# Two linear-attention and two gated layers on one core: adjacent token rows per partition, a new start, and an instruction order given by a table

## The chip, the cores and the metric

The kernel runs on one core of a Trainium2 chip. The metric is the time of one execution on the device in microseconds (us). A core has five engines, each with its own queue that is worked in order: TensorE (PE; its weight loads are PEld), VectorE (DVE), ScalarE (ACT), GpSimd (POOL) and SyncE (SP), which here issues most DMAs.

## The reference

```python
x = A_x                                              # 1 x 2048 x 512, bf16
x = x + _A_ref(_layernorm(x), wqkv, w_phi, wo)       # linear attention, 32 heads of 16
x = x + _B_ref(_layernorm(x), W_gate, W_up, W_down)  # gated layer, 1376 hidden columns
x = x + _A_ref(...)                                  # the same weights once more
x = x + _B_ref(...)

# _A_ref
pq, pk = q @ w_phi, k @ w_phi                        # per head
phi_q = concat([softmax(pq), softmax(-pq)])          # phi_k in the same way, of pk
kv, z = phi_k^T v, sum over tokens of phi_k
o = (phi_q kv) / (phi_q z + 1e-6);  return o @ wo
# _B_ref
gate = gate * (gate > 0);  return (gate * up) @ W_down
```

Nothing in it depends on the order of the tokens: the layer norm, the projections and the gated layer work row by row, and the attention sums over all rows.

## The kernel before, in words

The 2048 tokens are 16 tiles of 128 rows; x stays in SBUF in `x_sb` from the load to the store. `build_kernel` doesn't emit instructions in program order. It records each step as an operation (`Program.op`, L59) with its engine, the data it reads and writes, and two assumed durations, and then calls `schedule` (L299). That function gives each operation a priority (`tails`, L120: the longest chain behind it), plays all five queues forward (`forward`, L129: among the operations that could start within 60 ns, the one of the highest priority goes first), derives new priorities by a backward pass, does so 8 times and keeps the order with the smallest assumed length. DMAs have assumed costs as well (L52, L53). `prepare` (L314) turns the order into semaphore waits, and `emit` writes each engine's queue. So a change to an assumed cost can move instructions everywhere. At run time each queue is worked in the order thus fixed.

The start: DVE builds an identity matrix (L444 to L459). Partition p of `x_sb` holds rows p, 128 + p, and so on (`xv`, in the view `b (t p) d`). The key weights are loaded in four blocks (L494), transposed on TensorE (L527), copied out of PSUM (L532, L534), multiplied by a block-diagonal form BD of w_phi (L518, L542) and copied to `Wkp` (L546, L548), so that one projection gives pk. The same is done for the queries (`Wqp`), whose transposed weights come by four DMA transposes (L485) on SP. Five matmuls on a zeroed tile (L514) stand at the head of TensorE's queue.

The layer norm `ln` takes statistics on DVE (L559, L560), the reciprocal root as ln and exp on ACT (L562, L564), and y = normalised x on DVE (L579) or, for tiles 4 to 15 of the first layer (`POOL_Y`), on POOL (L574, L576). y is transposed either on TensorE with a copy by ACT (L588, L591; the tiles in `PE_Y`) or by a DMA transpose on SP (L594). `kv_tile` makes K (L612), two exponentials on ACT (L617), their sums z on DVE (L618), their reciprocals (L622, L623 on ACT or L625 on DVE), the product on DVE (L626), and V (L635) with its copy on ACT (L638). `kv_sums` multiplies phi_k and V over all tiles (L671), and DVE takes the wanted blocks (L679, L682). `q_chunk` makes Q (L651) and its exponentials (L655). `attn_tile` makes the attention of a tile: the product with the sums (L704), the denominators over ACT (L718, L727, L728) and POOL (L725, L726, L729), the scaling on DVE (L738, L743, L747), the transpose (L753 or a DMA, L759), the projection (L764) and the addition to x (L767). The gated layer makes gate and up columns (L794), the relu on ACT (L801), the product hT on DVE (L802), a remainder of 96 columns (`rem`, L822 to L831), and the down projection (L846, L848) with the addition to x (L852). Tiles of the last layer are stored by SP (L854). All eight PSUM banks are one pool, handed out by `forward`.

SP's queue at the start holds, in this order: the four key blocks, x tiles 2 and 3, the value weights, x tiles 4 to 7, the four weight transposes, x tiles 8 to 11, x tiles 12 to 15, and then the y transposes. ACT issues x0, w_phi and x1.

Of the kernel before, what the change touches and what calls it, by code (L numbers as in the profile page):

```python
# [10 lines left out]
P = 128  # L11
# [38 lines left out]
class Program:  # L50
    SYNC = 40.0
    DMA_ISSUE, DMA_FIXED, DMA_BW = 520.0, 1500.0, 230.0  # L52
    TR_ISSUE, TR_FIXED, TR_TIME = 1250.0, 1050.0, 250.0  # L53

    def __init__(self, n_dma_sems=64):
        self.ops = []
        self.n_dma_sems = n_dma_sems
# [41 lines left out]


# [12 lines left out]
    def lat(self, o):  # L113
        if o.dma == "tr":
            return self.TR_ISSUE + self.TR_FIXED + self.TR_TIME
        if o.dma:
            return self.DMA_ISSUE + self.DMA_FIXED + o.nbytes / self.DMA_BW
        return o.lat

    def tails(self):  # L120
        tail = [0.0] * len(self.ops)
        for o in reversed(self.ops):
            best = self.lat(o)
            for s, data in o.succ:
                best = max(best, tail[s.i] + (self.lat(o) + self.SYNC if data else self.busy(o)))
            tail[o.i] = best
        return tail

    def forward(self, prio, look=60.0):  # L129
# [4 lines left out]
        for o in ops:  # L134
            o.npend = len(o.deps) + len(o.order)
            o.ready = 0.0
            o.prio = prio[o.i]
            for t in o.tiles:
                tiles[id(t)] = t
# [3 lines left out]
        free = dict.fromkeys(ENGINES, 0.0)  # L143
# [32 lines left out]
        while left:  # L176
# [45 lines left out]
            if o.dma == "tr":  # L222
                free[e] = st + self.TR_ISSUE
                bus = max(bus, free[e]) + self.TR_TIME
                o.end = bus + self.TR_FIXED
            elif o.dma:
                free[e] = st + self.DMA_ISSUE
                bus = max(bus, free[e]) + o.nbytes / self.DMA_BW
                o.end = bus + self.DMA_FIXED
            else:  # L230
                free[e] = st + o.ii
                o.end = st + o.lat
# [66 lines left out]
    def schedule(self, rounds=12):  # L299
        self.links()  # L300
        prio = self.tails()
        best = None
        self.log = []
        for k in range(rounds):
            m = self.forward(prio)
            self.log.append(m)
            if best is None or m < best[0]:
                best = (m, prio)
            prio = self.backward([o.start for o in self.ops])
        self.forward(best[1])  # L310
        return best[0]
# [66 lines left out]
def build_kernel(nc, A_x, A_wqkv, A_w_phi, A_wo, B_x, B_W_gate, B_W_up, B_W_down, out):  # L378
# [8 lines left out]
    def sb(name, shape, dt=BF16):  # L387
        return E(nc.sbuf_tensor(name, [P] + list(shape), dt))
# [13 lines left out]
    rowi, coli, colf = sb("rowi", [32]), sb("coli", [32]), sb("colf", [1], FP32)  # L402
# [41 lines left out]
    op("dve", lambda e: e.memset(wm.ap(), 0.0), writes=[c_warm], ii=150, lat=210, name="warm")  # L444
    op("dve", lambda e: e.memset(ident[:], 0.0), writes=[c_id], ii=60, lat=100, name="id0")
    op("dve", lambda e: e.memset(rowi[:, 0:1], 0.0), writes=[c_row], ii=30, lat=70, name="row0")
    for k in range(5):
        n = 1 << k
        op("dve", lambda e, n=n: e.tensor_scalar(rowi[:, n:2 * n], rowi[:, 0:n], float(n), None, ALU.add), reads=[c_row], writes=[c_row], ii=70, lat=150, name="row")
    op("dve", lambda e: e.transpose(coli[:], rowi[:]), reads=[c_row], writes=[c_col], ii=100, lat=215, name="col")  # L450
    c_colf = res("colf")
    op("dve", lambda e: e.tensor_copy(colf[:], coli[:, 0:1]), reads=[c_col], writes=[c_colf], ii=70, lat=150, name="colf")
    c_idq = [res("identq", q) for q in range(4)]
    for q in range(4):
        sl = slice(32 * q, 32 * q + 32)
        op("dve", lambda e, sl=sl: e.tensor_scalar(ident[sl, sl], rowi[sl, :], colf[sl, :], None, ALU.is_equal), reads=[c_row, c_colf, c_id], writes=[c_idq[q]], ii=75, lat=150, name="identq")
    c_id = c_idq
    op("dve", lambda e: e.tensor_reduce(m8[:], ident[:].rearrange("p (h d) -> p h d", d=16), AX.X, ALU.add), reads=c_id, writes=[c_m8], ii=200, lat=290, name="m8")
    op("dve", lambda e: e.tensor_reduce(mask2[:].rearrange("p (a b) -> p a b", b=2), ident[:].rearrange("p (a f b) -> p a b f", f=16, b=2), AX.X, ALU.add), reads=c_id, writes=[c_m2], ii=200, lat=290, name="mask2")  # L459
    op("dve", lambda e: e.memset(eps[:], 1e-5), writes=[c_eps], ii=35, lat=70, name="eps")  # L460
    va_all = p_va.slots
    for i in range(16):
        op("pool", lambda e, i=i: e.memset(va_all[i][:, :, 128:130], 1.0), writes=[res("va1", i)], ii=60, name="vones")
    for i in range(2):
        op("pool", lambda e, i=i: e.memset(p_hr.slots[i], 0.0), writes=[res("hr0", i)], ii=500, name="hr0")
    op("pool", lambda e: e.tensor_copy(kvs[:, :, 136:144], mask2[:].unsqueeze(1).to_broadcast([P, 8, 8])), reads=[c_m2], writes=[res("kvsm")], ii=200, lat=280, name="kvsm")


    xv = A_x.rearrange("b (t p) d -> p (b t) d", p=P)
    outv = out.rearrange("b (t p) d -> p (b t) d", p=P)  # L470
# [13 lines left out]
    def load_wT(dst, rr, col, ic):  # L484
        o = op("sp", lambda e: e.dma_start_transpose(dst.ap()[:, :, ic * 128:(ic + 1) * 128], A_wqkv[ic * 128:(ic + 1) * 128, col:col + 512]),  # L485
               writes=[rr[ic]], dma="tr", nbytes=131072, name=f"wT{col}.{ic}", after=chain["sp"][-1:])
        chain["sp"].append(o)
# [5 lines left out]
    def load_wk(ic):  # L493
        load("sp", lambda e: e.dma_start(wk_n[ic][0].ap(), A_wqkv[ic * 128:(ic + 1) * 128, 512:1024]), [wk_n[ic][1]], 131072, f"wk{ic}")  # L494
    load_x("act", 0, 1)
    load_wk(0)
    load("act", lambda e: e.dma_start(w128[:], A_w_phi.rearrange("(c h) d f -> (h d) c f", c=4)), [c_w128], 16384, "wphi")
    load_wk(1)
    load_wk(2)
    load_x("act", 1, 2)  # L500
    load_wk(3)
    load_x("sp", 2, 4)
# [5 lines left out]
    load_x("sp", 8, 12)  # L508
    load_x("sp", 12, 16)
# [3 lines left out]
    for k in range(5):  # L513
        op("pe", lambda e: e.matmul(pt_w.ap(), wm.ap()[:, 0:128], wm.ap(), start=True, stop=True), reads=[c_warm], writes=[r_w], ii=430, lat=600, name="warm")  # L514


    for a in range(4):
        op("dve", lambda e, a=a: e.tensor_tensor(BD[:].rearrange("p c (a f b) -> p c a f b", f=16, b=2)[:, :, a], w128[:].unsqueeze(3).to_broadcast([P, 4, 16, 2]),  # L518
                                                 m8[:, 2 * a:2 * a + 2].unsqueeze(1).unsqueeze(1).to_broadcast([P, 4, 16, 2]), ALU.mult),
           reads=[c_w128, c_m8], writes=[c_BD[a]], ii=190, lat=280, name="BD")  # L520

    for ic in range(4):
        pt, pres = tile(p_ps, "WkT", ic)

        def mmt(e, ic=ic, pt=pt):
            for c in range(4):
                i = e.transpose(pt.ap().bitcast(BF16)[:, c * 128:(c + 1) * 128], wk_n[ic][0].ap()[:, c * 128:(c + 1) * 128], ident[:])  # L527
            return i
        op("pe", mmt, reads=[wk_n[ic][1]] + c_id, writes=[pres], ii=240, lat=400, name="WkT mm")
        src = lambda pt: pt.ap().bitcast(BF16)[:, 0:512].rearrange("p (c n) -> p c n", c=4)  # L530
        if ic % 2:
            op("act", lambda e, ic=ic, pt=pt: e.activation(t_wk.ap()[:, :, ic * 128:(ic + 1) * 128], src(pt), ACT.Copy), reads=[pres], writes=[c_wkT[ic]], ii=477, lat=580, name="WkT cp")  # L532
        else:
            op("dve", lambda e, ic=ic, pt=pt: e.tensor_copy(t_wk.ap()[:, :, ic * 128:(ic + 1) * 128], src(pt)), reads=[pres], writes=[c_wkT[ic]], ii=340, lat=420, name="WkT cp")  # L534
# [15 lines left out]
    r_wk = compose(t_wk, c_wkT, Wkp, "Wkp", ["act", "dve", "act", "dve"])  # L550
# [5 lines left out]
    def ln(l, ts):  # L556
# [9 lines left out]
        for t in ts:  # L566
# [6 lines left out]
            if (l, t) in POOL_Y:  # L573
                op("pool", lambda e, t=t: e.tensor_scalar(nmr[:, t, :], mv[:, t, 0:1], rstd[:, t, :], -1.0, ALU.mult, ALU.mult), reads=[res("mv", t), res("rstd", t)], writes=[res("nmr", t)],  # L574
                   ii=100, lat=170, name=f"nmr{l}.{t}")
                op("pool", lambda e, t=t, yt=yt: e.tensor_scalar(yt.ap(), x_sb[:, t, :], rstd[:, t, :], nmr[:, t, :], ALU.mult, ALU.add), reads=[res("x", t), res("nmr", t), res("rstd", t)],  # L576
                   writes=[yr], claims=[dst], ii=1000, lat=1050, name=f"yp{l}.{t}")
# [15 lines left out]
            else:  # L593
                op("sp", lambda e, yt=yt, dst=dst, c=c: e.dma_start_transpose(dst.ap()[:, :, c:c + 128], yt.ap()), reads=[yr], writes=[rr],  # L594
                   dma="tr", nbytes=131072, name=f"yT{l}.{t}")
# [5 lines left out]
    def kv_tile(l, t):  # L601
# [12 lines left out]
        kop[l, t] = op("pe", mmk, reads=[rr] + r_wk, writes=[kr], claims=[ft], ii=864, lat=1030, name=f"K{l}.{t}")  # L614
# [73 lines left out]
    def attn_tile(l, t):  # L688
# [69 lines left out]
        else:  # L758
            op("sp", lambda e: e.dma_start_transpose(oT_.ap(), ot_.ap()), reads=[or_], writes=[oTr], dma="tr", nbytes=131072, name=f"oT{l}.{t}")  # L759
# [46 lines left out]
    def rem(l, s):  # L806
# [7 lines left out]
        for k in range(2):  # L814
# [17 lines left out]
           dma="tr", nbytes=131072, name=f"remT{l}.{s}")  # L832
# [24 lines left out]
    for g in ([0], [1], [2], [3], [4, 5], [6, 7], [8, 9, 10, 11], [12, 13, 14, 15]):  # L857
        ln(0, g)
    for t in range(NT):
        kv_tile(0, t)  # L860
    last_tr = [o for o in pr.ops if o.name.startswith("yT0.") and o.dma]
# [28 lines left out]
    pr.schedule(ROUNDS)  # L890
# [18 lines left out]
ROUNDS = 8  # L909
ACT_RZ = {(0, t) for t in range(16)} | {(2, t) for t in range(0, 16, 2)}  # L910
POOL_Y = {(0, t) for t in range(4, 16)}
PE_Y = {(0, 0), (0, 1), (0, 2), (1, 0), (1, 1), (2, 15), (3, 0), (3, 1)}
# [44 lines left out]
```

## Time and profile before

| | |
|---|---|
| time, median of 13 runs | 398.09 us (396.31 to 398.67) |
| the profiled execution's own time | 398.0 us |
| its span, first instruction to last | 396.2 us |
| TensorE, busy | 381.0 us |
| DVE, ACT, POOL busy | 283.4, 199.4, 45.0 us |
| DMA | 23.02 MB, mean 58 GB/s |
| key blocks landed (L494) | 3.38, 3.95, 6.12, 6.58 us |
| K of tile 0 done, first z on DVE (L618) | 14.6, 16.2 us |
| last phi_k product of the first layer (L626), end | 53.7 us |

Times are counted from the first instruction. A row of the timeline is a start, a duration, the engine, the line, the operation, what it writes and reads with the shapes, and how many such instructions were merged; in brackets stands how long the engine had been idle and for whom it had waited. Matmuls overlap: each is recorded with its whole latency, so the pace of TensorE is read from the distance of their starts. Some matmul records are missing, so a full stretch of 10 us reads about 9.95 us busy.

### The profile page before, as it was taken

To read this page: it belongs to the slowest core of one execution; us is meant where nothing else is said; L and a number is where in the kernel's file an instruction comes from. 1 tells how busy PE (TensorE), PEld (TensorE's weight loads), DVE (VectorE), ACT (ScalarE), POOL (GpSimd) and SP (SyncE) were. 2 spreads that over 40 slices of the span, in tenths; PEclk is the share of its full clock that TensorE was granted. 3 is DMA by queue.
4 is the path that set the end of the run, shared out by engine and by line. 5 is a ranking of instruction groups with operands and counts; after the bars stand their busy time and mean duration, and the time that the engine had idled before them with its cause. 6 is when DMAs were issued, how large, how long until landed. Compare 5 with 4: busy or idle time off the path is not lost.

```text
span 396.2 us, 6502 instructions
## 1 busy us (share of the span) xinstructions
PE 381.0 (96%) x2362; PEld 209.8 (53%) x2405; DVE 283.4 (72%) x599; ACT 199.4 (50%) x615; POOL 45.0 (11%) x143
## 2 busy tenths in 40 slices
PE   6979999899999999999999999989999999999996
PEld 3434755677655444444444466567765544444442
DVE  8898957998889636545699993799888962433424
ACT  4789779765444204303149966976544420303300
POOL 2174012221111000000000001222111100000000
PEclk9999999999999999999999999999999999999999
DMA  8655920134221402002022000014423140110012
GB/s 224 163 95 133 345 72 13 35 76 80 51 57 28 80 15 40 14 2 40 15 41 53 2 2 2 15 32 76 80 52 59 27 79 15 40 38 17 0 48 73
DMA packets 63439, 23.02 MB, mean 58 GB/s; under 512 B 54352, under 2 KB 63408, under 8 KB 63408
## 3 DMA queue, kind: packets, MB, share of 16 engines
q1 hardware_dynamic: 62592, 22.33, 24.8%
q8 instruction: 19, 0.31, 0.3%
q10 hardware_dynamic: 816, 0.28, 0.3%
q14 instruction: 12, 0.10, 0.1%
HBM read 7.91 MB, written 2.10 MB: 25 GB/s over the span
## 4 chain that ended last, share of the span: by engine, by line
PE 72%; ACT 12%; DVE 9%; POOL 2%; issue 2%; DMA 1%; POOLq 0%
PE pb L794 30%; PE pb L846 17%; PE pb L635 6%; ACT expq L655 5%; PE pb L764 4%; PE pb L671 4%; PE pb L612 4%; ACT phik L617 3%; PE pb L651 2%; PE pb L822 2%; PE pb L848 2%; DVE stats L559 2%; PE pb L704 2%; DVE t L738 1%; ACT sm L718 1%
## 5 line engine op out<-in xcount | busy, mean ns | idle before, releaser
L801 ACT ACTIVATE gate<-pb 128x512 bf16<-128x512 f32 (+1 forms) x100 | 50.7, 509 | 101.5 <-PE pb L794 100.9
L794 PE MATMUL pb<-yT,Wg 128*128 128x512 bf16 (+1 forms) x395 | 83.0, 336 | 0.3
L794 PE MATMUL pb<-yT,Wu 128*128 128x512 bf16 (+1 forms) x393 | 82.5, 336 | 0.4
L802 DVE TENSOR_TENSOR hT<-gate,pb 128x512 bf16<-128x512 bf16 (+1 forms) x100 | 56.2, 573 | 35.6 <-PE pb L794 35.2
L846 PE MATMUL pb<-Wd,hT 128*128 128x512 bf16 x310 | 73.6, 379 | 0.4
L794 PEld LDWEIGHTS pb<-yT,Wg 128*128 128x128 bf16 x400 | 37.7, 98 | 33.1 <-DVE hT L802 1.6
L794 PEld LDWEIGHTS pb<-yT,Wu 128*128 128x128 bf16 x400 | 38.3, 98 | 28.1 <-DVE hT L802 0.5
L846 PEld LDWEIGHTS pb<-Wd,hT 128*128 128x128 bf16 x320 | 31.2, 98 | 38.0
L852 DVE TENSOR_TENSOR x_sb<-x_sb,pb 128x512 bf16<-128x512 bf16 x32 | 21.8, 682 | 37.4 <-PE pb L848 37.3
L559 DVE BATCH_NORM_STATS2 stats<-x_sb 128x6 f32<-128x512 bf16 x64 | 43.0, 684 | 0.4
L618 DVE TENSOR_REDUCE z<-phik 128x64 f32<-128x1024 bf16 x32 | 37.5, 1206 | 3.4 <-ACT phik L617 1.7
L655 ACT ACTIVATE expq<-pb 128x512 bf16<-128x512 f32 x64 | 35.0, 608 | 8.7 <-PE pb L651 8.7
L738 DVE TENSOR_TENSOR t<-pb,sm 128x384 bf16<-128x384 f32 x64 | 32.6, 548 | 7.7 <-POOL sm L729 6.9
L617 ACT ACTIVATE phik<-pb 128x512 bf16<-128x512 f32 x64 | 35.6, 641 | 4.0 <-PE pb L612 4.0
L562 ACT ACTIVATE lnv<-mv,eps 128x1 f32<-128x1 f32 (+2 forms) x56 | 16.4, 298 | 41.3 <-DVE mv L560 41.3
L725 POOL TENSOR_TENSOR sm<-sm 128x64 f32<-128x64 f32 x32 | 10.5, 329 | 225.5 <-ACT sm L718 225.5
L612 PE MATMUL pb<-Wkp,yT 128*128 128x512 bf16 x124 | 30.2, 385 | 2.4 <-DMA yT<-y 2.0
L767 DVE TENSOR_TENSOR x_sb<-x_sb,pb 128x512 bf16<-128x512 bf16 x32 | 21.7, 677 | 14.2 <-PE pb L764 14.2
L764 PE MATMUL pb<-wo,oT 128*128 128x512 bf16 x120 | 30.5, 379 | 0.6
L651 PE MATMUL pb<-yT,Wqp 128*128 128x512 bf16 x122 | 29.7, 380 | 1.3 <-DVE t L738 0.8
L635 PE MATMUL pb<-wv,yT 128*128 128x512 bf16 x125 | 30.6, 387 | 0.2
L579 DVE TENSOR_SCALAR y<-x_sb,mv,rstd 128x512 bf16<-128x512 bf16 x52 | 21.1, 409 | 3.3 <-ACT rstd L564 3.3
(69 smaller groups left out, 387.1 us busy)
## 6 DMA issues: line engine op xcount, KB each, us to landing
out_dram<-x_sb SPq DMA_DIRECT2D x16, 128.0 KB, 1.7
x_sb<-in_A_x_dram SPq DMA_DIRECT2D x3, 512.0 KB, 5.2
Wg<-in_B_W_gate_dram SPq DMA_DIRECT2D x2, 640.0 KB, 7.6
Wu<-in_B_W_up_dram SPq DMA_DIRECT2D x2, 640.0 KB, 8.5
Wd<-in_B_W_down_dram SPq DMA_DIRECT2D x1, 1280.0 KB, 12.5
yT<-y SPq DMA_TRANSPOSE x56, 2.5
hT<-in_A_wqkv_dram SPq DMA_DIRECT2D x4, 128.0 KB, 3.6
wv<-in_A_wqkv_dram SPq DMA_DIRECT2D x1, 512.0 KB, 6.0
```

The costliest lines, as they stand in the source:

```text
L559: op("dve", lambda e, t=t: e.bn_stats(stats[:, t, :], x_sb[:, t, :]), reads=[res("x", t)], writes=[res("st", t)], ii=600, lat=690, name=f" ...
L612: i = e.matmul(kt.ap(), src.ap()[:, ic, c0:c0 + 128], Wkp[:, ic, :], start=(ic == 0), stop=(ic == 3))
L617: op("act", lambda e, s=s: e.activation(ft.ap()[:, s, :], kt.ap(), ACT.Exp, scale=(1.0, -1.0)[s]), reads=[kr], writes=[fr2[s]], ii=477, la ...
L618: op("dve", lambda e: e.tensor_reduce(zt.ap().rearrange("p (a b) -> p a b", b=2), ft.ap().rearrange("p s (a f b) -> p (s a) b f", f=16, b= ...
L635: i = e.matmul(vt.ap(), src.ap()[:, ic, c0:c0 + 128], wv[:, ic, :], start=(ic == 0), stop=(ic == 3))
L651: i = e.matmul(qt.ap(), Wqp[:, ic, c * 128:(c + 1) * 128], src.ap()[:, ic, :], start=(ic == 0), stop=(ic == 3))
L655: op("act", lambda e, g=g: e.activation(es[g][0].ap(), qt.ap(), ACT.Exp, scale=(1.0, -1.0)[g]), reads=[qr], writes=[es[g][1]], ii=477, lat ...
L764: i = e.matmul(wt.ap(), oT_.ap()[:, c, :], wo[:, c, :], start=(c == 0), stop=(c == 3))
L794: i = e.matmul(pt.ap()[:, 0:n], W[:, ic, fc * 128:(fc + 1) * 128], src.ap()[:, ic, a * 128:b * 128], start=(ic == 0), stop=(ic == 3))
L801: op("act", lambda e: e.activation(st_.ap()[:, 0:n], gt.ap()[:, 0:n], ACT.Relu), reads=[gr], writes=[sr], ii=110 + n * .72, lat=230 + n * ...
L802: op("dve", lambda e: e.tensor_tensor(ht.ap()[:, a * 128:b * 128], st_.ap()[:, 0:n], ut.ap()[:, 0:n], ALU.mult), reads=[sr, ur], writes=[h ...
L846: i = e.matmul(pt.ap(), hT[l, s, fc].ap()[:, c:c + 128], Wd[:, fc, :], start=(fc == 0), stop=False)
```

## The change

Six things are changed. (1) The view of x and of the output: partition p now holds the 16 adjacent rows 16p to 16p + 15. (2) The start: x0 moves to the head of SP's queue and x1 behind the key blocks; ACT issues w_phi and the first key block; rowi is made by eight memsets and two steps; two of the four BD products move to POOL, with POOL's memsets behind them; the copies of the transposed key weights and of `Wkp` swap engines; K of tile 0 is four operations that each wait for their own quarter of `Wkp`; `first` adds to the priorities of all that K of tiles 0 to 3 needs. (3) The five matmuls on a zeroed tile become 40 of 128 columns. (4) The loads of x tiles 8 to 11 and 12 to 15 stand behind the DMA transposes of tiles 4 and 6. (5) y of tiles 4 and 5 moves from POOL to DVE, y of tile 3 is transposed on TensorE, and the layer norm groups of the first layer are pairs. (6) The assumed costs are other ones, and the priorities come from a table in the source, `RANKS` (one number per operation), with a single forward pass. The resulting order differs on every engine. K and V of twelve tiles of the third layer and 16 of its Q matmuls now stand within the second layer.

```diff
-    SYNC = 40.0
-    DMA_ISSUE, DMA_FIXED, DMA_BW = 520.0, 1500.0, 230.0
-    TR_ISSUE, TR_FIXED, TR_TIME = 1250.0, 1050.0, 250.0
+    SYNC, START = 40.0, 750.0
+    DMA_ISSUE, DMA_FIXED, DMA_BW = 470.0, 1600.0, 240.0
+    TR_ISSUE, TR_FIXED = 1250.0, 750.0
...
+    def first(self, goals, step):
+
+        for k, g in enumerate(goals):
+            stack = [g.i]
+            while stack:
+                i = stack.pop()
+                if i not in self.boost:
+                    self.boost[i] = (len(goals) - k) * step
+                    stack += self.ops[i].deps + self.ops[i].order
...
+    def behind(self, o, first):
+
+        o.order.append(first.i)
...
-            o.prio = prio[o.i]
+            o.prio = prio[o.i] + self.boost.get(o.i, 0.0)
...
-    def schedule(self, rounds=12):
+    def schedule(self, rounds=12, ranks=None):
         self.links()
+        if ranks is not None:
+            self.boost = {}
+            return self.forward([float(r) for r in ranks])
...
-    xv = A_x.rearrange("b (t p) d -> p (b t) d", p=P)
-    outv = out.rearrange("b (t p) d -> p (b t) d", p=P)
+    xv = A_x.rearrange("b (p t) d -> p (b t) d", p=P)
+    outv = out.rearrange("b (p t) d -> p (b t) d", p=P)
...
-    load_x("act", 0, 1)
-    load_wk(0)
-    load("act", lambda e: e.dma_start(w128[:], A_w_phi.rearrange("(c h) d f -> (h d) c f", c=4)), [c_w128], 16384, "wphi")
+    load_x("sp", 0, 1)
+    load("act", lambda e: e.dma_start(w128[:], A_w_phi.rearrange("(c h) d f -> (h d) c f", c=4)), [c_w128], 65536, "wphi")
+    load_wk(0, "act")
     load_wk(1)
     load_wk(2)
-    load_x("act", 1, 2)
     load_wk(3)
+    load_x("sp", 1, 2)
     load_x("sp", 2, 4)
...
-    for k in range(5):
-        op("pe", lambda e: e.matmul(pt_w.ap(), wm.ap()[:, 0:128], wm.ap(), start=True, stop=True), reads=[c_warm], writes=[r_w], ii=430, lat=600, name="warm")
-
+    for k in range(WARM):
+        op("pe", lambda e: e.matmul(pt_w.ap()[:, 0:128], wm.ap()[:, 0:128], wm.ap()[:, 0:128], start=True, stop=True), reads=[c_warm], writes=[r_w], ii=107 if k < 30 else 56, lat=300, name="warm")
...
-    r_wk = compose(t_wk, c_wkT, Wkp, "Wkp", ["act", "dve", "act", "dve"])
+    r_wk = compose(t_wk, c_wkT, Wkp, "Wkp", ["dve", "act", "dve", "act"])
...
+        if (l, t) == (0, 0):
+            for ic in range(4):
+                o = op("pe", lambda e, ic=ic: e.matmul(kt.ap(), src.ap()[:, ic, c0:c0 + 128], Wkp[:, ic, :], start=(ic == 0), stop=(ic == 3)),
+                       reads=[rr, r_wk[ic]], writes=[kr], claims=[ft], ii=216, lat=382, name=f"K{l}.{t}")
+            kop[l, t] = o
...
-    for g in ([0], [1], [2], [3], [4, 5], [6, 7], [8, 9, 10, 11], [12, 13, 14, 15]):
+    for g in ([0], [1], [2], [3], [4, 5], [6, 7], [8, 9], [10, 11], [12, 13], [14, 15]):
         ln(0, g)
...
+    for k, o in enumerate(late_x):
+        pr.behind(o, next(d for d in pr.ops if d.name == f"yT0.{4 + 2 * k}"))
...
-    pr.schedule(ROUNDS)
+    pr.first([kop[0, t] for t in range(FIRST)], 1e5)
+    ranks = None
+    if RANKS:
+        raw = base64.b85decode("".join(RANKS))
+        ranks = struct.unpack(f"<{len(raw) // 2}H", raw)
+        assert len(ranks) == len(pr.ops)
+    pr.schedule(ROUNDS, ranks)
...
-POOL_Y = {(0, t) for t in range(4, 16)}
-PE_Y = {(0, 0), (0, 1), (0, 2), (1, 0), (1, 1), (2, 15), (3, 0), (3, 1)}
+POOL_Y = {(0, t) for t in range(6, 16)}
+WARM = 40
+FIRST = 4
+PE_Y = {(0, 0), (0, 1), (0, 2), (0, 3), (1, 0), (1, 1), (2, 15), (3, 0), (3, 1)}
```

With the table given, `first` and `tails` set nothing: `schedule` clears the additions and uses the table alone. The lines of the changed kernel that the text below speaks of: L640 and L644 are K, L669 V, L836 hT.

## The prediction

> **What bounds the kernel now.** I read the page first, then busy time by stretches, TensorE's waits, the merged timeline of the first 76 us, and the order of instructions of both programs. The page and TensorE's waits:
>
> ```profile
> span 396.2 us, 6502 instructions
> PE 381.0 (96%) x2362; PEld 209.8 (53%) x2405; DVE 283.4 (72%) x599; ACT 199.4 (50%) x615; POOL 45.0 (11%) x143
> PE   6979999899999999999999999989999999999996
> ...
> PE pb L612 <- DMA yT<-y: 2.0, 2, 1.3
> PE pb L588 <- ACT expq L655: 1.6, 2, 0.8
> PE pb L514 <- DVE gate L444: 1.4, 1, 1.4
> PE pb L651 <- DVE t L738: 0.8, 2, 0.4
> ```
>
> TensorE is the bound, and there is little idle time to win back. Stretches of 10 us tell where it lies (first PE, then PEld, DVE, ACT, POOL, granted clock, DMA share, GB/s):
>
> ```profile
> 50.00:60.00 10.00, 9.53 (x85) 5.85 (x85) 5.58 (x14) 8.36 (x26) 1.74 (x6) 1.00 0.17 54
> 60.00:70.00 10.00, 9.87 (x69) 5.46 (x69) 7.16 (x17) 9.24 (x30) 1.79 (x6) 1.00 0.07 13
> 70.00:80.00 10.00, 8.91 (x81) 6.69 (x82) 9.37 (x26) 7.42 (x32) 2.67 (x9) 1.00 0.22 42
> ...
> 210.00:220.00 10.00, 9.95 (x50) 4.69 (x50) 10.00 (x13) 10.00 (x25) 0.00 (x0) 1.00 0.13 26
> ```
>
> 9.95 is a full stretch (a missing record makes the rest). From 100 to 240 and from 290 to 380 us nearly every stretch reads so: nothing can be won there. Against 9.95, 50 to 100 us lack 0.42 + 0.08 + 1.04 + 0.19 + 0.08 = 1.8 us (attention of the first layer: projections wait until DVE, ACT and POOL have normalised), and 240 to 290 us lack 0.42 + 0.71 + 0.47 + 0.15 + 0.09 = 1.8 us (attention of the second). The stretches 20 to 30 us lack 5 - 4.20 + 5 - 3.71 = 2.1 us: the two waits of L612 for transposed y. The rest is the start, where busy time misleads (start, duration, then the group):
>
> ```profile
> 1.40 2.32 PE L514 MATMUL pb<-gate 128*128 128x512 bf16 x5 [1.40 <-DVE gate L444]
> 10.97 1.91 PE L635 MATMUL pb<-wv,yT 128*128 128x512 bf16 x4
> 14.80 1.03 PE L612 MATMUL pb<-Wkp,yT 128*128 128x512 bf16 x4
> 16.24 1.22 DVE L618 TENSOR_REDUCE z<-phik 128x64 f32<-128x1024 bf16 x1 [1.75 <-ACT phik L617]
> 11.94 23.77 SPq L594 DMA_TRANSPOSE yT<-y  x13
> ```
>
> Four matmuls of 512 columns take 1.91 us at 11 us and 1.03 us at 14.8 us. Less the last one's latency (0.63 and 0.38) they start 0.43 and 0.22 us apart: TensorE runs at half speed until about 14.7 us, though the clock column reads 1.00. K of tile 1 (L612 at 14.80) starts when V0, K0 and three transposes of y (tiles 0 to 2) are done.
>
> **The change part by part.**
>
> *Token layout and loads.* A partition now takes adjacent token rows, so a four-tile load has pieces of 4 KB and a one-tile load or a store pieces of 1 KB, 16 KB apart in DRAM. The page counts all but 31 of 63439 packets below 2 KB, and one slice moved 345 GB/s with those: I cost the larger pieces at nothing. Bounds: half the 4.4 us of an x load (issued 10.77, landed 15.20) would still be no gain at the start, as the first tiles are alone in their loads; a store landed in 1.7 us and only the last one counts, so at worst a few tenths are lost.
>
> *First keys first.* SP now issues x0, wk1, wk2, wk3, x1; ACT issues w_phi, then wk0. The last of the four key blocks landed at 6.58 (the fourth load of L494); one 128 KB load fewer stands ahead, so I take 6.4. From there the path is: four transposes 0.6, copy 0.42, then DVE in its new order: Wkp copy 0.66, statistics of tile 1 0.60, Wkp copy 0.68, which gives 9.4; the last two quarters of K0 start at 9.4 and 9.83 and end at 10.45. Before, K0 ended at 14.6, behind V0: this is the part that does what it says. But K1 doesn't follow at once. TensorE's order is K0, V0, yT1, yT2, K1, and y2 stands on DVE behind the first z (L618). exp of K0 on ACT is done at 11.55, z at 12.75, y2 at 13.1, its transposes put K1 at about 13.4. The ACT route agrees: two exp (11.55), two ln and two exp of tiles 2 and 3 (0.75), va0 (0.6), yT1 copy (0.6) give 13.5. So K1 moves from 14.80 to 13.4: 1.4 us, with the same work done. If the landings are half a us earlier, 1.9; if z or va0 is late, 0.9.
>
> *TensorE kept busy.* Five matmuls of 512 become 40 of 128, 30 of them ahead of the first weight transposes. At half speed 512 columns are 0.43 us apart, so 128 are 0.107: 30 take 3.2 us from about 1.1, to 4.3 us; the first weight transposes started at 4.35 before. The ten others (1.1 us at most) lie in waits for the blocks. Cost nothing while those waits cover them; 0.3 us if the blocks land early. Does it raise the clock? [...] In this trace full speed came 4.2 us after TensorE became dense at 10.6. [...] The sum hardly differs: V0 at half speed costs 0.86 more, and that falls into the wait for y2. Only if the clock stays down past K1 is it paid: K1, V1, K2, V2 at 0.86 each, at most 3.4.
>
> *Wait of 20 to 30 us.* It comes from late transposes: y of tiles 4 and 5 were last on POOL (from 18.04, behind a late rstd), x8 and x12 stood ahead of the first transpose. Now y4 and y5 are DVE's, x8 goes behind the transpose of tile 4 and x12 behind that of 6, and Q of the first four tiles (12 matmuls, 2.6 us) and the Wqp products (0.7) stand between. From 13.4: K1, yT3, V1, K2, V2, products, K3, V3 put K4 at 19.8; y4 at 17.2 plus 2.5 (median from issue to landing) is 19.7. yT5 is behind x8's 512 KB (19.0 + 4.3 = 23.2, then 0.7 as the transpose at 11.94 landed 0.7 after such loads): 23.9, wanted at 24.1. x8 landed, statistics, then POOL's pairs (2.02 us per pair) give yT8 at 29.5, wanted at 30.2. So the 2.1 us go, with little margin: 0.5 to 1 may return at each of the three. One more tile is transposed on TensorE: 0.25.
>
> *What is late next: DVE.* From the first z it must do 16 z (1.14 each), 16 products (0.60), 12 statistics (0.60), aggregates, four y and two Wqp copies: 18.2 + 9.6 + 7.2 + 0.8 + 1.3 + 1.2 = 38.3 us. Before, from 16.24 to 53.7, it had four statistics and four y fewer to do and 3 us idle. From 11.55 it ends at 49.9 without idle; with 1.5 us idle, at 51.4 instead of 53.7: 2.3 us earlier. TensorE alone would gain 1.4 + 2.1 - 0.25 = 3.2. I take 2.5 us at the end of the kv sums, 1 to 4 as the range.
>
> *POOL's BD products.* Nearest rows: POOL 64 elements 329 ns, 32 elements 276 ns, so 128 about 0.43 us each, two 0.9 us, beside DVE, from the landing of w_phi (4.1 before): done by 5, ahead of the copy that the product waits for anyway. Nothing; 0.3 if the first POOL product is slow. The memsets behind them (2 us) are wanted by va0 at 12. Identity: eight memsets in place of three dependent steps save some 0.5 us before 4.3, covered by the warm-up.
>
> *Searched order.* From the kv sums to the first gate columns the new order has the same 44 Q, 48 R, 16 transpose and 16 projection matmuls in each layer, only spread otherwise, with the two y transposes apart instead of together (they waited 1.6 us for expq). The chain behind is a latency that doesn't get shorter; I take two thirds of 1.8 + 1.8, 2.4 us. Ends: nothing, and 3.6. K and V of twelve tiles of layer 2, and 16 Q matmuls, move into the gated layer, where TensorE is full (9.95) before and after: nothing won. What DVE does for them (z, product, reciprocal, 2 us per tile) now stands ahead of the hT products that free banks. DVE had 5 to 6 of 10 us busy there, and four pairs of banks cover 4 x 1.73 = 6.9 us: nothing, up to 0.5 per tile.
>
> Sum: 2.5 + 2.4 = 4.9 us. The profiled run took 398.0 (span 396.2 and 1.8 around it), the median is 398.1. The tail of 3.9 us behind the last matmul stays. Forecast 393.2.
>
> **The rivals.**
> 1. *All waits go*: start 3.2, both attentions 3.6, and the clock rises early, which takes z and y2 off the path for 1.5 more: 8.3 us, 389.8. For it: beside each attention wait there are Q matmuls enough (44, 9.5 us) to fill it. Against it: DVE.
> 2. *The start alone*: attention waits are chains and stay, 2.5 us: 395.6.
> 3. *Slower*: DVE takes TensorE's place in the gated layer. If each of 16 moved tiles of K, V holds up a bank for 0.5 us more than it is covered, 8 us are lost, less 4.9 won: 401. It decides from 0.3 us per tile. For it: a fixed order on in-order queues, and z (1.2 us) ahead of hT products, several times two or three of such steps together. Against it: 40% of DVE was free there.
> 4. *It doesn't do what it says*: wk3 lands no earlier, yT5 and yT8 wait behind the loads: the 2.1 us come back, the rest 0.3: 398, no change.
>
> **How the numbers follow.** Forecast 0.45; rival 1 0.20; rival 2 0.16; rival 3 0.12; rival 4 0.07. A measurement can tell some 0.2% (0.8 us) from no change. Rival 4 is split between same and either side: faster 0.82, same 0.05, slower 0.13. The range runs from 389.0, just beyond rival 1, to 398.2, which takes in rivals 2 and 4 and leaves rival 3 out.
>
> **What would show it.** K of tile 1 at 13.4 (12.9 to 14) and its matmuls 0.22 us apart; first z at 11.5; no wait of L640 (K in the changed kernel) for yT over 0.5 us; the last product of layer 1's keys at 51.4; TensorE in the two attentions lacking 1.2 instead of 3.6 us; stretches in the gated layers at 9.95. I am wrong if those show waits for hT (L836), if matmuls are 0.43 us apart past 15 us, or if the first z is no earlier.

## The result, and the profile after

The changed kernel takes 393.65 us (median of 11 runs, 391.23 to 394.68) against 397.9 us before (median of 48 runs): the ratio is 0.989, 95% interval 0.9873 to 0.9907. The forecast was 393.2. The profiled execution has a span of 391.7 us, 4.5 less. Page and TensorE's waits of the changed kernel:

```profile
span 391.7 us, 6568 instructions
PE 378.7 (97%) x2403; PEld 211.2 (54%) x2444; DVE 288.7 (74%) x602; ACT 204.2 (52%) x620; POOL 42.5 (11%) x141
PE   7899999999999999999999999999899999999996
```

```profile
PE pb L798 <- DMA oT<-o: 1.3, 1, 1.3
PE pb L616 <- DVE y L607: 1.2, 1, 1.2
```

The waits for transposed y that the kernel before had between 20 and 30 us are gone; the largest wait is a new one, for a transposed o. The start, from the timeline (start, duration, group):

```profile
1.08 3.38 PE L536 MATMUL pb<-gate 128*128 128x128 bf16 x30 [1.08 <-DVE rowi L473]
4.79 0.39 PE L555 MATMUL pb<-ident,hT 128*128 128x128 bf16 x4
9.34 1.04 PE L669 MATMUL pb<-wv,yT 128*128 128x512 bf16 x4
10.37 1.22 DVE L652 TENSOR_REDUCE z<-phik 128x64 f32<-128x1024 bf16 x1
11.97 0.40 PE L616 MATMUL pb<-ident,y 128*128 128x128 bf16 x4 [1.19 <-DVE y L607]
12.20 1.03 PE L640 MATMUL pb<-Wkp,yT 128*128 128x512 bf16 x4
```

Four transposing matmuls take 0.39 us from 4.8 us on (0.61 to 0.63 before), V0 1.04 us at 9.34 (1.91 at 10.97 before): the clock, read from this pace (its column reads 1.00 throughout), is up from about 4.3 us. K of tile 1 starts at 12.20, the first z at 10.37; before it was 14.80 and 16.24. The matmuls of the first layer's sums end at 51.4 us instead of 55.0. Stretches of 10 us (PE first):

```profile
50.00:60.00 10.00, 9.52 (x85) 5.91 (x85) 5.27 (x15) 7.68 (x27) 2.47 (x8) 1.00 0.55 182
60.00:70.00 10.00, 9.56 (x67) 4.99 (x66) 8.58 (x20) 9.48 (x33) 2.24 (x7) 1.00 0.15 29
...
210.00:220.00 10.00, 9.95 (x47) 4.49 (x46) 8.18 (x13) 4.99 (x12) 0.00 (x0) 1.00 0.07 15
280.00:290.00 10.00, 8.70 (x75) 6.75 (x75) 8.05 (x20) 4.27 (x18) 1.87 (x6) 1.00 0.25 55
```

Against 9.95, 50 to 100 us (five such stretches) now lack 1.4 us and 240 to 290 us lack 2.2 us: 3.6 in all, as before. The gated layers are still full. So in this execution most of the gain is made at the start: 3.6 of the 4.5 us are there when the sums end, 0.9 come behind them. What the order wins behind the sums is larger than 0.9; late transposes take part of it back, as the experiments show.

### The profile page after: what moved, and what is told of

It is laid out like the page before. It is cut to its first block, busy times and chain, and to the rows that moved or that the text cites. A ratio compares the mean times of both kernels' runs of the same rounds, so it can differ in the third digit from the quotient of the medians.

```text
span 391.7 us, 6568 instructions
## 1 busy us (share of the span) xinstructions
PE 378.7 (97%) x2403; PEld 211.2 (54%) x2444; DVE 288.7 (74%) x602; ACT 204.2 (52%) x620; POOL 42.5 (11%) x141
## 4 chain that ended last, share of the span: by engine, by line
PE 71%; DVE 18%; ACT 5%; DMA 3%; issue 1%; POOL 1%; SPq 0%
PE pb L828 31%; PE pb L880 16%; PE pb L798 5%; DVE z L652 5%; PE pb L640 4%; PE pb L669 3%; DVE stats L587 3%; ACT expq L689 3%; DVE phik L660 3%; PE pb L685 2%; PE pb L705 2%; PE pb L856 2%; PE pb L738 2%; PE pb L882 2%; DMA oT<-o 2%; DVE t L772 1%
## 5 line engine op out<-in xcount | busy, mean ns | idle before, releaser
L836 DVE TENSOR_TENSOR hT<-gate,pb 128x512 bf16<-128x512 bf16 (+1 forms) x100 | 56.8, 574 | 35.6 <-PE pb L828 33.9
L828 PE MATMUL pb<-yT,Wg 128*128 128x512 bf16 (+1 forms) x393 | 80.9, 336 | 0.4
L880 PE MATMUL pb<-Wd,hT 128*128 128x512 bf16 x311 | 75.0, 379 | 0.7 <-DMA hT<-hr 0.2
L689 ACT ACTIVATE expq<-pb 128x512 bf16<-128x512 f32 x64 | 36.1, 611 | 8.7 <-PE pb L685 8.6
L772 DVE TENSOR_TENSOR t<-pb,sm 128x384 bf16<-128x384 f32 x64 | 33.9, 546 | 1.1 <-POOL sm L763 0.8
L669 PE MATMUL pb<-wv,yT 128*128 128x512 bf16 x126 | 32.1, 379 | 0.3
L685 PE MATMUL pb<-yT,Wqp 128*128 128x512 bf16 x123 | 30.7, 380 | 1.7 <-DVE t L777 0.5
L640 PE MATMUL pb<-Wkp,yT 128*128 128x512 bf16 x120 | 30.8, 379 | 0.2
L590 ACT ACTIVATE lnv<-mv,eps 128x1 f32<-128x1 f32 (+1 forms) x58 | 16.7, 295 | 26.8 <-DVE mv L588 26.2
L752 ACT ACTIVATE sm<-pb 128x48 f32<-128x48 f32 (+1 forms) x96 | 16.6, 214 | 20.3 <-PE pb L738 19.9
```

The source lines that it names most:

```text
L640: i = e.matmul(kt.ap(), src.ap()[:, ic, c0:c0 + 128], Wkp[:, ic, :], start=(ic == 0), stop=(ic == 3))
L669: i = e.matmul(vt.ap(), src.ap()[:, ic, c0:c0 + 128], wv[:, ic, :], start=(ic == 0), stop=(ic == 3))
L685: i = e.matmul(qt.ap(), Wqp[:, ic, c * 128:(c + 1) * 128], src.ap()[:, ic, :], start=(ic == 0), stop=(ic == 3))
L689: op("act", lambda e, g=g: e.activation(es[g][0].ap(), qt.ap(), ACT.Exp, scale=(1.0, -1.0)[g]), reads=[qr], writes=[es[g][1]], ii=477, lat ...
L772: return e.tensor_tensor(tt_.ap()[:, b, 0:384].rearrange("p (c h d) -> p c h d", h=8, d=16), pt.ap()[:, 0:432].rearrange("p (c w) -> p c w ...
L828: i = e.matmul(pt.ap()[:, 0:n], W[:, ic, fc * 128:(fc + 1) * 128], src.ap()[:, ic, a * 128:b * 128], start=(ic == 0), stop=(ic == 3))
```

## The experiments

Each kernel was timed beside the kernel before. The first z (us), the end of the first layer's sums, and TensorE's waits behind 30 us for tiles transposed by DMA, summed from the waits' brackets in the timeline, are from the profiled execution. That is one execution; with the loads on the old queues, for instance, it took 391.96 us, 1.9 less than the median.

| kernel | time, us | ratio to before, 95% interval | first z | sums end | such waits |
|---|---|---|---|---|---|
| changed | 393.65 | 0.9873 to 0.9907 | 10.37 | 51.42 | 1.5 |
| without the table | 394.33 | 0.9891 to 0.9943 | 10.72 | 52.41 | 0.6 |
| old token layout | 393.39 | 0.9858 to 0.9908 | 10.71 | 51.72 | 2.3 |
| narrow warm-up | 394.2 | 0.9874 to 0.9941 | 10.80 | 51.81 | 2.1 |
| stores last | 393.15 | 0.9855 to 0.9915 | 11.35 | 52.36 | 0.4 |
| loads on old queues | 393.86 | 0.9871 to 0.9927 | 10.87 | 51.93 | 0.7 |
| x loads ahead | 393.28 | 0.9868 to 0.9931 | 10.30 | 52.58 | 2.3 |
| y2 first | 394.31 | 0.9889 to 0.9946 | 11.14 | 52.80 | 2.7 |
| y2 first, copy first | 394.41 | 0.9908 to 0.9964 | 10.81 | 52.46 | 3.1 |
| y4, y5 on POOL | 394.37 | 0.9907 to 0.9967 | 10.65 | 53.06 | 0.2 |
| 18 instructions more | 396.64 | 0.9956 to 0.9997 | 11.01 | 52.07 | 5.1 |
| before, keys raised | 398.88 | 1.0014 to 1.0054 | 14.11 | 55.14 | 0.4 |
| no table, keys not raised | 397.55 | 0.9984 to 1.0018 | 15.70 | 54.47 | 0.7 |

**Theory and rivals at first.** From the profile after, my theory was that the start made the gain, and that the table gave in the attentions with one hand what it took with the other, by stores put between transposes. Rivals: the table makes the gain; the layout makes it; the warm-up makes it. Four kernels tell them apart.

*Without the table.* The order comes from the list again, with the new costs and the raised keys:

```diff
-RANKS = (
-    'A_xWu2M8euCI~190tf>LD+me*F9*H{VFob>DF_e-Tn7^f8VCsp;0G26=m#SRBnT%6IR}si9|#f$&jk+#B?u}8{swmk0RYzr_X4K}_y+|9(FZOB)CRl<$pqd7',
...
-)
+RANKS = ()
```

> The changed kernel with the order table emptied: the priorities are derived again from the longest chains, with the additions for the first four K and the best of 8 rounds; layout, loads, warm-up, engines and assumed costs stay. Theory A (the start made the gain, the searched order adds little: at equal work TensorE stalled 3.6 us in the second attention before and after, 3.6 and 2.7 in the first): 393.5 to 395.3. Rival B (the table is worth two thirds of the gain or more): 396.5 or later. Rival C (the order hurts, as the new 1.3 us wait for a transpose of o shows): below 393.

It has all but 0.7 us of the gain: the table is not its main source, as far as these intervals can tell.

*Old token layout.*

```diff
-    xv = A_x.rearrange("b (p t) d -> p (b t) d", p=P)
-    outv = out.rearrange("b (p t) d -> p (b t) d", p=P)
+    xv = A_x.rearrange("b (t p) d -> p (b t) d", p=P)
+    outv = out.rearrange("b (t p) d -> p (b t) d", p=P)
```

> The changed kernel with the old token layout (partition p holds rows p, 128 + p, ...), the same order on every engine. Theory A (pieces of 1 KB move as fast as those of 4 KB, and nobody waits for the x loads): within 0.4 us of the changed kernel. Rival B (larger pieces bring x8 and x12, and the key blocks beside them, earlier): 1 to 3 us slower, with landings over 0.5 us later.

The layout is worth nothing that can be measured.

*Narrow warm-up*: the 40 matmuls have 8 columns, so TensorE is nearly idle until the first key block.

```diff
...
-pt_w.ap()[:, 0:128], wm.ap()[:, 0:128], wm.ap()[:, 0:128]
+pt_w.ap()[:, 0:8], wm.ap()[:, 0:128], wm.ap()[:, 0:8]
...
```

> The changed kernel with its 40 zero matmuls on 8 columns instead of 128, in the same places: TensorE is nearly idle before the key blocks land. Theory A (keeping TensorE busy raises the clock at about 4.4 us, and without it the clock rises 3 to 4 us into the dense work, near 13): matmuls of K0 and V0 0.43 us apart, K of tile 1 at 13 to 13.6 instead of 12.2, 0.8 to 2.5 us slower. Rival B (the clock rises by itself with the transposes and products): no difference, within 0.3 us.

The timeline of this kernel, the same steps as above:

```profile
3.73 0.61 PE L555 MATMUL pb<-ident,hT 128*128 128x128 bf16 x4 [1.69 <-DMA hT<-in_A_wqkv_dram]
8.38 1.26 PE L644 MATMUL pb<-Wkp,yT 128*128 128x512 bf16 x3 [0.24 <-issue]
```

The clock is still at half speed at 8.4 us (of the three matmuls in the second row the first takes 634 ns, the last 380) and full from 9.3: the warm-up does raise it some 5 us earlier. But the first z is only 0.4 us later, and the time is within the interval of the changed kernel's: the path to the first z runs over copies on ACT and DVE, and without the warm-up the first weight transposes begin 0.5 us earlier (3.73).

*Stores last.* In the changed order four stores stand between transposes on SP, one of them 0.4 us ahead of the late transposed o. Here they stand behind the last transpose.

```diff
+    tail = [o for o in pr.ops if o.eng == "sp" and o.dma == "tr" and o.name.split(".")[0] in ("yT3", "oT2", "remT3")]
+    for o in pr.ops:
+        if o.dma == "store":
+            for d in tail:
+                pr.behind(o, d)
```

> The changed kernel with all 16 stores on SP behind the last DMA transpose. Theory A (the transpose of o issued right behind a store at 277 us took 4.1 us to land instead of 2.4, and TensorE waited 1.3 us for it; others behind stores took 3.1): 1 to 1.5 us faster than the changed kernel, 391.9 to 392.7, if the last stores don't queue up. Rival B (the o was late on DVE anyway, the wait moves elsewhere): within 0.4 us. Rival C (12 stores against 16 at the end lengthen the tail): slower by up to 1 us.

The stretch around the late o, in this kernel:

```profile
280.00:290.00 10.00, 9.95 (x84) 7.60 (x84) 8.74 (x24) 5.03 (x21) 2.19 (x7) 1.00 0.29 55
```

The transposed o landed 2.4 us after its issue and nothing waits. It looked as if the store was the cause; the next runs contradict that.

**Second set: single edits in a fixed order.** From here on (except the last two kernels) the changed kernel's own order of every engine is kept, and only what is named is moved.

*Loads on old queues.*

```diff
+    for n, e in (("x0", "act"), ("wk0", "sp"), ("x1", "act")):
...
+        at[n][0].eng = e
```

> The changed kernel with every engine's order of work kept, and only the first loads put back on their old queues: ACT issues x0, w_phi and x1, SP the four key blocks. If the order of the loads is what brought K of tile 1 forward by 2.6 us, the last key block lands near 6.4 instead of 5.2, the last quarter of K0 starts near 10 instead of 8.6 to 9.6, K of tile 1 comes at 13.2 to 13.4 and the time is about 394.8 us. If it is the order of the work (keys of tile 0 ahead of V, quarters), K of tile 1 stays at 12.2 to 12.6 and the time at 393.6. x1 comes earlier here, which can give back some tenths.

The last key block landed at 6.34 us, later as expected, but the first z came only 0.5 us later and the time stayed: the order of the loads is not what counts. And although the stores stand where the change put them, the o that is issued 0.4 us behind a store lands after 2.5 us here.

*x loads ahead.*

```diff
+    s = [o for o in pr.sequence if o not in late_x]
+    k = s.index(at["wT0.3"][0]) + 1
+    pr.sequence = s[:k] + late_x + s[k:]
```

> The changed kernel with every engine's order kept, but the loads of x tiles 8 to 15 stand on SP ahead of all transposes of y again. If the spacing of the loads is what took away the 2.1 us of waits between 20 and 30 us, K of tiles 4 and 5 waits for its transposed y by 1 to 2 us and the time is 395 to 395.7. The rival: the loads are now issued near 11 us and have landed by 16 to 17, when the first transpose is issued (15.8), so nothing waits and the time stays at 393.6; then it was the earlier y of tiles 4 and 5 and the work put in between that removed the wait.

A stretch of this kernel, and from its timeline its one large wait for y:

```profile
20.00:30.00 10.00, 9.95 (x47) 4.42 (x47) 9.91 (x20) 10.00 (x30) 3.37 (x8) 1.00 0.26 53
```

```profile
40.69 1.04 PE L669 MATMUL pb<-wv,yT 128*128 128x512 bf16 x4 [1.78 <-DMA yT<-y]
```

From 20 to 30 us TensorE is full: spacing the loads did not take the old wait away. The 1.78 us at 40.7 belong to a transpose that landed 4.2 us after its issue, as the o at 280 us had. There is no store near it.

*y2 first*: stores last, and y of tile 2 ahead of the first z on DVE. *Copy first* has in addition the copy of the transposed tile 1 ahead of the copy of V0 on ACT (`hoist` moves an operation, with what it still needs, ahead of another).

```diff
+    hoist(["y0.2"], "Z0.0")
+    hoist(["yTcp0.1"], "va0.0")
```

> The changed kernel with the stores behind the last transposes (as in the run before with stores last, 393.15 us), and on DVE y of tile 2 ahead of the first z, all else in the same order. If y2 behind z sets the start of K of tile 1, as the prediction had it, K of tile 1 comes 0.7 to 1.2 us earlier after the first quarter of K0 and the time falls to 392.2 to 392.5. The rival: ACT's queue (ln and rstd of tiles 2 and 3, the copy of V0, the copy of the transposed tile 1, done at 11.91) ends only 0.25 us ahead of the present start (12.20), so no more than 0.25 is won, and the time stays within 0.3 of 393.1.

> As the run with y2 ahead of the first z, and on ACT the copy of the transposed tile 1 ahead of the copy of V0. If ACT's queue is what then holds K of tile 1, it comes 0.6 to 0.8 us earlier than in the changed kernel, and the time is 392.4 if TensorE sets the pace of the first layer up to the sums. If DVE sets it (z and products of 16 tiles, 1.22 and 0.67 us each, from the first z on, which starts later here), the sums end no earlier and the time stays near 393.1.

The first edit moved the wrong tile, and the second keeps it: the table takes tile 3 ahead of tile 2 on TensorE, so y of tile 3 is the one waited for, and it now stood behind a z that had been put off by y of tile 2. The wait of L616 grew from 1.2 to 1.9 us, a transpose of y that landed 4.0 us after its issue cost another 1.6 us at 40.9 (40.6 in the second), and the first layer's sums ended later. Neither can judge ACT's part. With the stores last, both again had late o's (0.8 us of wait at 281 us).

*y4, y5 on POOL.*

```diff
+    for n in ("y0.4", "y0.5"):
+        at[n][0].eng = "pool"
```

> The changed kernel with every engine's order kept, and y of tiles 4 and 5 on POOL again (one instruction each, 0.76 us by POOL's row of y) instead of DVE (0.33 each). In the changed kernel and its variants the last product of phi_k ended 39.4 to 39.5 us after the start of the first z, with DVE idle for 0.01 us between. If DVE sets the end of the first layer's keys, this distance falls to 38.8 and the sums end 0.6 us earlier, counted from the first z; the time is 393.0. If TensorE sets it, the distance stays near 39.4 with 0.6 us idle on DVE. The transposed y of tiles 4 and 5 comes 0.4 to 0.9 us later; if the move of these two to DVE was needed against the wait of 20 to 30 us, K of tile 4 waits by that much.

From the timeline of this kernel:

```profile
20.06 1.04 PE L640 MATMUL pb<-Wkp,yT 128*128 128x512 bf16 x4 [1.12 <-DMA yT<-y]
```

The wait for y of tile 4 is back, and with it 2.0 us of idle time on DVE (0.01 in the changed kernel). The sums end 42.4 us after the first z instead of 41.05. So the move of these two y is needed to remove the wait; relieving DVE of 0.65 us gains nothing if its input then comes late.

*18 instructions more.* With four kernels contradicting the store, I looked at what DMA ran while a transpose was late. DMA of the changed kernel from 277.3 to 281.5 us, then of the kernel with the stores last from 277.4 to 280 us (queue, packets, MB, share; then issues, with the median from issue to landing):

```profile
q1 hardware_dynamic: 708, 0.27, 55.0%
q8 instruction: 1, 0.02, 2.0%
...
oT<-o SPq DMA_TRANSPOSE x1, 4.1
```

```profile
q1 hardware_dynamic: 544, 0.13, 25.2%
...
oT<-o SPq DMA_TRANSPOSE x1, 2.4
```

In the late case one packet of instructions was fetched, in the other none. Queue 8 fetches 16 KB at a time, 19 times in the span, with 255 of TensorE's matmuls and weight loads between two fetches on the mean; I take them to be TensorE's. Queue 14 fetches 8 KB at a time, 12 times in the span. Over all fourteen traces, behind 60 us, where the last load of weights has landed: 111 transposes landed more than 3.0 us after issue, and 110 of them overlapped a fetch of 8 or 16 KB between 1.0 us after their issue and their landing (82 one of 16 KB, 28 one of 8 KB alone); 81 that overlapped one in that time were not late; of 915 without a fetch in it one was late, and it met one earlier. Of those 915, 861 met no fetch at all and landed within 2.6 us; 35 of these had a store under way beside them. So behind 60 us a fetch goes with every late transpose, a store alone with none. To test it, the fetches are shifted against the work:

```diff
+    def warm(e, n):
+        for j in range(n):
+            e.matmul(pt_w.ap()[:, 0:8], wm.ap()[:, 0:128], wm.ap()[:, 0:8], start=True, stop=True)
+        return e.matmul(pt_w.ap()[:, 0:128], wm.ap()[:, 0:128], wm.ap()[:, 0:128], start=True, stop=True)
...
+        op("pe", lambda e, k=k: warm(e, 9 if k == 0 else 0), reads=[c_warm], writes=[r_w], ii=107 if k < 30 else 56, lat=300, name="warm")
```

> The changed kernel with the same order, and nine more matmuls of 8 columns at the head of TensorE's queue, which shift its instruction fetches by 18 instructions, 2 us of TensorE's work. In the traces so far all transposes on SP that land more than 3 us after their issue (median 2.4) overlap a fetch of 16 KB of instructions, with the stores in between or not. If the fetch is the cause of the wait of 1.3 us for the transposed o at 280 us, the slow landing moves to another transpose, each that lands late again overlaps a fetch, and the wait of L798 for oT is gone or changed; the time is 392.5 to 394. If the store ahead of it is the cause, the same o lands 4.1 us after its issue and the wait stays at 1.3.

Not every late transpose had met a fetch of 16 KB, as stands there: in the changed kernel two of the weight transposes at the start (6.6 and 5.3 us from issue to landing) met none, and of its six behind 60 us four met one and two met one of 8 KB alone.

TensorE's waits behind 60 us, first of this kernel, then of the changed one, then with the stores last:

```profile
PE pb L802 <- DMA oT<-o: 3.8, 4, 1.4
PE pb L644 <- DMA yT<-y: 1.0, 1, 1.0
...
PE pb L884 <- DMA hT<-hr: 0.3, 1, 0.3
```

```profile
PE pb L798 <- DMA oT<-o: 1.3, 1, 1.3
...
PE pb L880 <- DMA hT<-hr: 0.2, 1, 0.2
```

```profile
PE pb L798 <- DMA oT<-o: 0.2, 1, 0.2
PE pb L880 <- DMA hT<-hr: 0.2, 1, 0.2
```

The time was outside what I expected: 396.64 us, 3.0 more than the changed kernel's, and the ratios' intervals do not meet. Nine tiny matmuls at 1 us cost 3 us. In the profiled execution waits for transposed tiles behind 60 us rose from 1.5 to 5.1 us, and 0.65 us came at the start (sums at 52.07), where the clock rose later; the two at 267.6 and 285.6 us (1.42 and 1.14) belong to transposes that landed 4.2 and 3.9 us after issue, each with a fetch inside (265.5 and 282.1). The store is not the cause; the fetch is. The late y of the kernel with the x loads ahead (issued at 36.4) has one inside as well, at 37.7 us. Where a fetch falls is not quite fixed even for one order: with one order on TensorE, the fetch near 280 us came after 3739 of its records (changed kernel) or after 3768 (stores last, old queues, x loads ahead). So these last three kernels need not have escaped the late o by their edits.

*Before, keys raised*: the kernel before with `first` alone. *No table, keys not raised*: the changed kernel without both.

```diff
+            o.prio = prio[o.i] + self.boost.get(o.i, 0.0)
+    pr.first([kop[0, t] for t in range(4)], 1e5)
```

```diff
-    pr.first([kop[0, t] for t in range(FIRST)], 1e5)
+RANKS = ()
```

> The kernel before with one thing added: the priorities of all that K of tiles 0 to 3 needs are raised, as the change does it. Loads, warm-up, token layout, costs and the rest stay. If the order of work at the start is what brought the gain, K0 is no longer behind V0 on TensorE, the first z starts 2 to 4 us earlier than 16.24, and the time is 395 to 396.5. If loads, warm-up and spacing carry the gain, the first z comes less than 1 us earlier, or DVE idles as much later and TensorE waits between 20 and 30 us as before, and the time stays at 397.5 to 398.5.

> The changed kernel without the table and without the raised priorities: order from the list with the new costs, all else (loads, warm-up, layout, spacing, quarters of K0) as changed. The run without the table alone had 394.33, with the first z at 10.72. If the raised priorities at the start are what brought the gain, the first z comes 1 to 3 us later, the first layer's sums end as much later, and the time is 395.3 to 397. If the other parts carry it, the time stays within 0.5 of 394.3.

The first z of the kernel without table and raised keys (10.72 without the table alone):

```profile
15.70 1.22 DVE L652 TENSOR_REDUCE z<-phik 128x64 f32<-128x1024 bf16 x1
```

With loads, layout, warm-up, costs and spacing as changed but the keys not raised, the time is that of before: 397.55, ratio 1.0001. Raising them (394.33) brings the first z 5.0 us forward and 3.2 us in time. Only 2.1 us of this are there when the sums end: the list gives other orders behind them too, so this pair does not test the start alone. Yet raising them in the old kernel is no gain (398.88, 0.3% slower): the first z comes 2.1 us earlier, but the sums end at 55.14 as they did at 55.0, while twelve statistics stand between the first and the second z on DVE and TensorE still waits 1.0 us for a transposed y at 22.5 us. So the raised keys make the gain together with other parts of the change. By the end of the sums, y of tiles 4 and 5 on DVE is one (1.4 us, above), though in time the kernel without it cannot be told from the changed one. The layout, the new queues of the loads, the spacing and the warm-up, each taken out alone, change nothing that these intervals show. The quarters of K0 and the swapped copies were not tried alone.

## Why the prediction was right, and where it was not

The total was right to 0.5 us, and the main reason, the start, was right. That it came so near is luck in part: the start gave 1.1 us more than forecast, late transposes took 1.5 us that the forecast did not have, and the two nearly cancel.

*Layout, loads, BD on POOL, gated layers: nothing.* Right. The old layout had 393.39 us. The BD products took 0.38 us each on POOL (0.43 estimated), ahead of their reader. The one wait of a matmul for hT that the profile lists took 0.2 us and was for a transposed hT, so rival 3 is out.

*First keys.* The mechanism is right (y behind the first z holds K of tile 1; it is tile 3's, not tile 2's), the size too small: the last key block landed at 5.18 us, not 6.4, the first z came at 10.37, not 11.5, K of tile 1 at 12.20, not 13.4. But the landing is not the reason that counts. Seven kernels have the dense warm-up and DVE's order up to the first z in common; in them the first z follows the clock:

| kernel | last matmul at half speed starts | last key block landed | first z |
|---|---|---|---|
| x loads ahead | 4.15 | 5.21 | 10.30 |
| changed | 4.25 | 5.18 | 10.37 |
| y4, y5 on POOL | 5.21 | 6.14 | 10.65 |
| old token layout | 5.32 | 5.71 | 10.71 |
| loads on old queues | 5.64 | 6.34 | 10.87 |
| 18 instructions more | 5.67 | 5.67 | 11.01 |
| stores last | 6.70 | 5.47 | 11.35 |

The last kernel and the changed one have the same order of work on every engine up to there, so the first z of one execution is uncertain by 1.0 us. The landings show no such order, and the 0.5 us by which the old queues seemed to put off the first z fits the later rise of their clock. My chain from the landing to the first z, reckoned at half speed, was 0.6 us too long for the old queues (4.53 for 5.15).

*Clock.* In the kernel before, full speed came 4.2 us after TensorE became dense at 10.6; behind the dense work from 9.4 us the same delay would have put it near 13.6, an estimate from that one trace. It came at 4.3 us here, 3.2 us after the dense warm-up began at 1.08. In the ten other kernels with the same dense work from 1.1 us the last matmul at half speed started at 3.7 to 7.0 us, 2.6 to 5.9 us behind that, so the 4.2 us are no fixed delay; the same four matmuls that took 0.39 us at 4.79 us in the changed kernel took 0.63 us with the stores last, where the clock was still down:

```profile
5.21 0.63 PE L555 MATMUL pb<-ident,hT 128*128 128x128 bf16 x4
```

That the sum hardly differs held for the narrow warm-up, 0.4 us later at the first z, where the weight transposes also began 0.5 us earlier. It did not hold for a late rise behind the dense warm-up: the first z is then up to 1.0 us later, where I had nothing up to K of tile 1.

*The wait of 20 to 30 us goes.* Right, and so is the step with y4 and y5. Putting the loads behind the transposes was not needed. And of the 2.1 us, 1.29 were not a late queue: the second of the two transposes landed 4.37 us after its issue with two instruction fetches inside (25.0 and 25.5 us). I had taken a collision for a queue.

*DVE is late next.* Right: from the first z to the last product it is busy without a gap (0.01 us idle, 2.93 before), 39.47 us; I had 38.3 of work and 1.5 idle. One stretch of it, before and after (DVE is third):

```profile
30.00:40.00 10.00, 9.95 (x47) 4.57 (x47) 8.77 (x11) 10.00 (x30) 3.98 (x5) 1.00 0.61 143
30.00:40.00 10.00, 9.83 (x46) 4.30 (x46) 10.00 (x13) 9.72 (x29) 4.76 (x10) 1.00 0.41 81
```

The end of the last product follows the first z by 39.4 to 39.5 us in all six kernels that keep DVE's order and let nothing come late. It came at 49.8 us, where I had 51.4. So the gain at the sums was 3.6 us where I had 2.5; the 1.1 us more are those by which the first z was earlier than forecast.

*Searched order, 2.4 us.* This term failed: I took two thirds of the attentions' waits to go, and the stretches of the two attentions lack 3.6 us as before. The step that was missing is what a late transpose costs. In the changed kernel's profiled run 1.3 us are lost to one transposed o, 0.2 to a transposed hT. The prediction had no such term because before had no such wait behind 60 us; where a fetch falls was not to be read from the order. Without these waits the order does win. Take from each span the end of the sums and the waits for transposed tiles behind 60 us: before leaves 396.2 - 55.0 = 341.2 us, the changed kernel 391.7 - 51.4 - 1.5 = 338.8, all ten kernels with the table 337.8 to 338.8, the one without the table 339.9. So the order is worth some 2.4 us behind the sums, and the 4.5 us of the two spans are 3.6 at the start and 2.4 behind it, less 1.5 for late transposes. Not all of the 2.4 lies where I put it: with the stores last, where hardly a fetch struck a waited-for transpose, the stretches of the attentions lack 1.1 and 0.8 us, 1.7 less than before.

What stays open: some 0.9 us of what the order wins behind the sums do not show in the stretches of the attentions, and missing matmul records (2403 beside 2444 weight loads) allow no finer split. Why the clock rises at a different time in each execution was not tested. Whether another offset of the fetches would make the kernel faster than 393 us was not tried; none of the versions run is measurably faster than the changed kernel.

## What to carry to other kernels

When a kernel's first phase is bound by an engine other than the one that the page calls busiest, time what starts that engine's unbroken work (here the first z on DVE): while DVE's order stayed and no input came late, its last product ended 39.4 to 39.5 us after it, whatever else was changed. A higher priority for the first result is worth what the engine behind it can do with the earlier start, and nothing if other work then piles up there. And before a late DMA is put down to its queue or its neighbours, look for what else the DMA engines carried at that moment.

## What was not expected of the hardware

Behind 60 us a DMA transpose during which instructions were fetched often landed late: a transpose took 2.4 us from issue to landing, and between 3.0 and 4.6 us in 82 of 122 cases that met a fetch of 16 KB (one packet on one queue, 0.9 to 1.7 us) and in 28 of 69 that met one of 8 KB alone. The changed kernel's trace has 19 fetches of 16 KB beside 2403 matmuls and 2444 weight loads. What they cost shows up as late transposes, and a shift of 18 instructions moved the kernel by 3.0 us (0.65 of them at the start, beside a later rise of the clock), where the whole change won 4.3.
